# An issue list with 88 of 2459 operations in other places: an S4D convolution and a Hedgehog attention on one core

## The chip, the cores and the metric

The kernel runs on one core of a Trainium2 chip. The metric is the device time of one execution in microseconds (us). The core has five engines with an instruction queue each, and each takes its queue in order: PE (TensorE, matrix multiplication; the loading of its weights is shown apart as PEld), DVE (VectorE), ACT (ScalarE), POOL (GpSimd) and SP (SyncE, which here only issues DMA transfers). PE writes its results to PSUM, which has eight banks; DVE and ACT evict them from there.

## The reference, cut to what matters

Two heads work on inputs of their own and their outputs stand side by side, 2048 rows of 576 + 576 columns, in float32. Head A is a long convolution: a kernel K is summed out of 128 exponentials per channel, and FFTs of twice the length convolve it with u. Head B is linear attention with 32 heads of 18 columns.

```python
dt = jnp.exp(log_dt)                                        # A
A = -jnp.exp(log_A_real) + 1j * A_imag
C = (C_real + 1j * C_imag) * dt[:, None]
P = jnp.exp((A * dt[:, None])[:, :, None] * pos[None, None, :])
K = 2.0 * jnp.einsum("dn,dnl->dl", C, P).real
Kf = jnp.fft.rfft(K, L2)
Uf = jnp.fft.rfft(u_t, L2)
y = jnp.fft.irfft(Uf * Kf[None, :, :], L2)[:, :, :L]        # + u * D_skip
...
qkv = x @ wqkv                                              # B, split into q, k, v and heads
pq, pk = q @ w_phi, k @ w_phi
phi_q = concatenate([softmax(pq), softmax(-pq)])            # phi_k alike
kv, z = phi_k^T v, sum of phi_k
o = (phi_q kv) / (phi_q z + 1e-6)
out = concatenate([y, o @ wo])
```

## The kernel before, in words

The program first records 2459 operations in a plan (`Plan.op`), each with its engine (some with an alternate engine), the tiles that it reads and writes, and a number. An operation is one instruction, or one block of matmuls, or one transfer. `Plan.run` then walks through a long string, `ORDER`, and emits the operations in the order of its words; so the string sets what stands behind what in the queue of each engine. In a word the digits are the number of the operation; a trailing `x` takes the alternate engine; `@` and digits give the PSUM banks of the tiles that are made there; `:n` puts n matmuls on a tile of zeros in front of the operation (line 249, `self.zero.t` against 256 columns; they change no result). The semaphores follow from which tile an operation reads and writes.

What the operations are, in the order in which they mostly come:

- "fold" (lines 370 to 380): w_phi is multiplied into the weights. Four matmuls (line 375) and one more (line 376) for each of four stage tiles, named e, kvb, cs and e again, loaded from wkT; the other operand is fT. ACT copies the product as the high half (`wh`), DVE subtracts it to get the low half (`wl`) (lines 379 and 380). Operation 7 is the first block of four, operation 8 the one more of the same stage tile, operation 29 the next one more; 9 is the ACT copy of 7. 381 and 383 are such a block and its copy for the query weights.
- 16 "key" tiles of 128 rows: the projections (line 307, 14 matmuls of 288 columns for a half, weights `wh`/`wl` and, for v, `vh`/`vl`; operations 331, 198, 199, 158 and 159 are such halves), the two softmaxes on DVE, ACT and POOL (lines 446 to 470), and "k4", 64 small matmuls of e with v (line 508; operations 190, 229, 324, 150 and 170). The last product of the softmax is line 322, e<-e,small.
- 18 pairs of "group", which make K: "g0", six matmuls of 64 rows (line 811), "g1", range reduction and sines (lines 787 to 798), "g2", three exponentials of PSUM on ACT (line 824; 1511 and 1512 are two of them), "g3", four products on DVE (lines 828 to 833), and "g4", small matmuls (line 843; 1225, 1263 and 1517). Operation 1460 is a shift of a phase in g1, which either POOL (line 789) or ACT (line 787) can do.
- the transforms: "u" of the input, "kfirst" of K, 16 "product" steps that multiply the two (line 926 and elementwise steps; 2287 is the matmul block of product 13, 2339 an elementwise one of product 15), and 16 "last" steps (line 988), whose operand zi or cs is read back from DRAM by SP (line 979; 2445 for "last" 14, 2452 for 15) and whose result `ot` is stored (line 992).
- 16 "query" tiles: projection, softmax, transposes on PE (lines 562 and 590), the product with kv (line 578), division (line 326, o<-psum,small), and the output projection. 745 is a sum in the softmax of one of them (line 455), 752 and 754 evict the transposes of query 9.

The tile pools are small (three tiles for e, five for cs and ub, two for ff and zi), so a transfer or an eviction often waits for an earlier reader. On PE, the queue interleaves all these stages.

Of the kernel before, what the change touches and what calls it, by code (L numbers as in the profile page):

```python
# [1005 lines left out]
0 1 2 4 5 1104 1092 1105 6 1106 1107 1108 7@2:26 1109 1192 27 1110 8 34 9 1073 1095 1093 1111 20 51 13 1112 1113 1114 992 11 29@0 1115 1003 344 28  # L1006
36@6 35 21@4 12 30 37 52 1096 39 22 32 10 23 25 1094 44 15@2 1127 1116 1074 14 31 38 40 33 1004@06 1099 24 53 18 26 54 16 1154 19 1117 1137 287 1120
345 45 17 57@4 1075 1118 41 346x 1076 1077 56 46 1119 60 347 47 288 42 1078 289x 1005 349@2 1080 348 1121 290x 1122 61 1123 1124 1125 292@4 62 1161
291 1098 68 48 1126 1084 1128 268 43 1129 350@0 1396 1063 1138 1130 1006 1139 1131 1132 71 49 295 1133 1134 296 1400 1079 352 353 63 1135 58@6 1136 59
1081 55 3 64 354 1155 65 66 1082 351 1162 1156 69 67 72 355x 1085 1086 1140 73x 293@2 1157 50@4 1163 1193 361 1064@60 1007 269 1158 1194 356 1159 270x  # L1010
1083 70 297 271 74 1087 1097 294 298 1066 171 1088 304 1089 357 1164 299 300 77@0 358 301 272@2 1160 273 1165 303 1090 1399 276 1065 1091 1166 277 360
278 1401 1397 76 1199 111 1167 1200 80 302 1195 1147 1398 1168 1402 172 1141 274@2 359x 275 173x 305 1196 1142 81 1148 1197 362 174 1152@76 1201 82
279 1169 1170 1151@05 83x 285 1172 1067 1202 1171 1174 112 1203 113 79@2 1143 1175 1204 78 1180 75 1173 1068 280 1176 114 1177 1183 89 284 176@0
1153@23 1205 84 1198 1178@5 1149 85 325 1182 281 1181 1230 1207 86 175 1403 1038 177 1206 1231 1232 1179 282 1208 1233 115 283x 180 1234 117@6 1184
1185 116 286 1235 1186 1187@2 211 1048 181 120 179@0 1190@53 182 121 183 1237 326 1218 1150 87x 1238 1018 1221 1189@67 122 1188 178 327 1239 1209 1404
212 189 1211 328x 123x 88 118@2 330@0 119 213x 124 1210 1212 1213 1191@67 90 184 214 1214 129 1215 185 1220 188 1240 1144 1241 1216@5 1242 216@2 215
1145 1146 306 1269 91 1243 128 1236 1223 186 1268 187x 1224 1219 1222 92 1217 93 1405 1270 1271 331@6 219 220 94 332 1100 329 221 222 125 190 126 1419
1245 1406 333 1225@5 342x 1276 1275 1272 1277 1227@23 1244 1278 1246 1228@67 1247 334 127x 1249 1256 1226x 1248 191 335 223 218@0 1250 1252 1251 1253
217 1279 192 1280 193 130 1254@5 1273 307 228 1274 1259 336 194 1307 1049@20 1306 224 225 1051 1050x 341 1308 96@6 1282 1229@01 337 1281 1257 1258 97
1407 1262 338 197@2 339 100 101 196 1261 1260 199@6 308x 1052 1283 1284 198 226x 195 1412 227 1408 1409 1410 1411 1413 1255 200 1414 229 201 340x 1101  # L1020
# [5 lines left out]
318 254@0 1354 379x 133x 1333@62 1334 1335 1449 134 1439 151 1336 319 241 242 320 253 321x 1494 1495 246 1496 1497 257 258 256@6 1337@20 1338 259 1339  # L1026
324 1356@5 1499 1341@02 1343x 1453 1340 1489 260 243 244 152 153 154 1342 1490 1454 1455 255 266 261 1345@20 1344 1347 1346 136@6 1498 137 156@0 262
263 245 265 1348 140 141 1500 142 1019@26 1021x 424 157 1450 1020x 135 998 264x 267 160 1481@67 1501 1482@23 1503 1502 161 1504 143 1456 168 1457 162
144 248 1458 1459 163 1451 1461x 138@0 1507 164 1008 139 1506 1505 145 165 149 1357 1508@2 1452 363 999@60 380 1460x 1509 1510 1483@52:2 1000 382@6
1001x 381 383 146 1513 148 1511 1512 1002 1514 1515 166 158@0 401 147x 1516 385 159 384 169x 150 1517@5 167x 1518x 170 1034@20 1522 1523 1524 1525 386  # L1030
1526 366 1036x 1529 1443@54:2 1527 1530 1531 1532 1528 1533 1534 1462 1463 1022 1009@06:2 1011 1464 1035x 1444@23:4 403@6 1466 1467 402 1535 1445@54
1465 1472 1010 406 1468 404 394 1473 1043 1537 387 458 1469 1474 395@0 1536 1429 1470@2 396 408 1037 405 407 1471 1475 1476 389@6 388 1478 1477 1361
1362 397 392 365 390 409@2 399 410 1363 1364 1365 1366 411 1367 391 1479@5 1368 1369 1370 1371 1372 412 1480x 1430 1373 1374 413 400 414 367@4 393
371@5 368x 1013 994@62 398 995x 372x 1375x 1012 415 459@0 364 374x 996x 369x 460 373x 370x 461 462 463 375 1431 997 426@3 425 1538 1432 1376 416 417
1433 1044@16:2 1434 464 1435 1688 376 377 427 428 1377 1519@50:2 1539 1046 1045x 1520@41:2 155 1436 1541 429 526 492 418 465 1540 1542 1014@62:8 1545
1544 1521@54:4 1548 1437 430 1438 466 1543 431 432 1546@0 1653 1016 1550 1654 1549 1692 1551 1547 527@2 467 528 1655 1656 433 468 434 469 378 1015 419
435 436 439@1 1657 441@7 1554 437@0 470 1658 1552 1553 1358@56 440 1028 1555@4 1047 442 1659 1691 438 1378 1556 446@7 1379 1359@14 529 530 1667 531
1387 1381 1380 1382 447 448 1360@03 1661 1383 532 443@2 444 1660 1662 1384 1663 1388 1689 471@5 493@6 1664 533 445 1665 1690 1666 1668 534 1390 535
1385@2 472 1389 1386 473@5 449@14 475@2 420 474 1577 1391 450 536 1392 476 537 1393 421 538 494 495 451 496 480@5 1578 1017 1394@0 477@1 1395x 1579
# [68 lines left out]
```

## Time and profile before

| | us |
|---|---|
| median of 3 runs | 534.08 |
| lowest and highest | 532.86 and 534.81 |
| the profiled execution | 532.96 |
| span of its trace | 531.2 |
| PE busy / DVE busy | 516.0 / 450.5 |
| ACT busy / POOL busy | 381.2 / 344.3 |

The span is from the first instruction to the last; 1.8 us of the profiled execution lie around it. The mean granted clock of PE is 0.999 of full speed over the span. A row of the trace gives a start, a duration, engine, line and operation, and in brackets how long the engine was idle before it and what ended that. Matmuls overlap their neighbours, so the durations of single rows add up to more than the time between starts.

### The profile page before, as it was taken

How to read it: one execution, taken by the hardware profiler on the slowest of the kernel's cores; microseconds unless marked ns; L12 is line 12 of the kernel's file. 1: busy time of each engine (PE TensorE's matmuls, PEld its weight loads, DVE VectorE, ACT ScalarE, POOL GpSimd, SP SyncE). 2: the span in 40 equal slices, each digit the busy share in tenths (PEclk: the TensorE clock that was granted, in tenths of full speed). 3: DMA queues.
4: the chain of work that ended last, by engine and by line, in shares of the span. 5: the costliest groups of instructions: out<-in, count | busy, mean ns of one | idle time of the engine just before them, and what ended most of it. 6: DMA issues, size and time to landing. Idle time of an engine off the chain costs nothing.

```text
span 531.2 us, 19221 instructions
## 1 busy us (share of the span) xinstructions
PE 516.0 (97%) x8179; PEld 432.3 (81%) x8179; DVE 450.5 (85%) x705; ACT 381.2 (72%) x559; POOL 344.3 (65%) x483
## 2 busy tenths in 40 slices
PE   8999999999999899999999999999999999999997
PEld 7998999988988778988888666866788876776986
DVE  7999989797958798999999998999974899768641
ACT  6679979889568699899699978989733444354342
POOL 1167877957687957983659998896541526673233
PEclk9999999999999999999999999999999999999999
DMA  8836610425155666446762687765368699897884
GB/s 288 308 121 233 222 52 27 168 78 198 51 161 179 213 235 245 127 139 192 271 210 83 197 266 233 254 212 182 102 206 289 204 283 301 271 298 253 271 292 148
DMA packets 69900, 107.10 MB, mean 202 GB/s; under 512 B 5722, under 2 KB 49882, under 8 KB 69814
## 3 DMA queue, kind: packets, MB, share of 16 engines
q1 hardware_dynamic: 69174, 104.39, 60.3%
q0 software_dynamic: 640, 1.48, 0.9%
q8 instruction: 64, 1.05, 0.8%
q14 instruction: 22, 0.18, 0.1%
HBM read 61.30 MB, written 44.54 MB: 199 GB/s over the span
## 4 chain that ended last, share of the span: by engine, by line
PE 72%; DVE 14%; DMA 4%; issue 4%; ACT 4%; POOL 1%; SPq 0%; DVEq 0%; ACTq 0%; POOLq 0%
PE psum L307 67%; PE psum L562 3%; DMA ff<-in_ff_dram 2%; DVE cs L829 2%; DMA zi<-dram 1%; PE psum L590 1%; ACT psum L824 1%; DVE ac L326 1%; DVE small L447 1%; DVE small L455 1%; DVE cs L326 1%; DMA pa<-in_par_dram 1%; DVE e L326 1%; DVE cs L831 1%; DVE small L450 1%
## 5 line engine op out<-in xcount | busy, mean ns | idle before, releaser
L307 PE MATMUL psum<-vh,x 128*128 128x288 f32 x576 | 123.6, 301 | 0.2 <-DVE e L326 0.2
L307 PE MATMUL psum<-wh,x 128*128 128x288 f32 x576 | 123.6, 301 | 0.1
L770 POOL TENSOR_TENSOR cs<-cs,pi 128x32 int32<-128x32 int32 (+4 forms) x180 | 106.7, 598 | 7.6
L307 PEld LDWEIGHTS psum<-wh,x 128*128 128x128 f32 x576 | 94.3, 188 | 7.3 <-issue 3.7
L307 PEld LDWEIGHTS psum<-vh,x 128*128 128x128 f32 x576 | 94.0, 188 | 4.8 <-issue 3.2
L307 PE MATMUL psum<-wl,x 128*128 128x288 f32 x320 | 93.8, 296 | 0.0
L307 PE MATMUL psum<-vl,x 128*128 128x288 f32 x320 | 93.8, 295 | 0.0
L824 ACT ACTIVATE psum<-psum 128x512 f32<-128x512 f32 x108 | 59.0, 586 | 8.7 <-PE psum L307 8.1
L307 PEld LDWEIGHTS psum<-wl,x 128*128 128x128 f32 x320 | 60.2, 188 | 0.0
L307 PEld LDWEIGHTS psum<-vl,x 128*128 128x128 f32 x320 | 60.2, 188 | 0.0
L322 POOL TENSOR_TENSOR e<-e,small 128x1152 f32<-128x1152 f32 (+1 forms) x26 | 44.7, 1719 | 18.1 <-DVE small L326 12.9
L828 DVE TENSOR_TENSOR cs<-psum,cs 128x1024 f32<-128x1024 f32 x36 | 43.7, 1216 | 6.0 <-ACT psum L824 5.8
L322 POOL TENSOR_TENSOR x<-zo,x 64x128 fp32r<-64x128 f32 (+1 forms) x33 | 26.4, 804 | 32.2 <-ACT x L407 30.8
L322 POOL TENSOR_TENSOR e<-small,e 128x576 f32<-128x576 f32 x28 | 32.7, 1167 | 18.4 <-PE psum L307 7.8
L307 PEld LDWEIGHTS psum<-kvb,fT 126*128 126x128 f32 (+1 forms) x320 | 38.6, 188 | 7.2 <-issue 3.0
L829 DVE TENSOR_TENSOR cs<-psum,cs 128x1024 f32<-128x1024 f32 x36 | 43.6, 1215 | 0.9 <-ACT psum L824 0.8
L307 PE MATMUL psum<-kvb,fT 126*128 126x133 f32 (+1 forms) x320 | 42.0, 280 | 0.3 <-DVE ac L326 0.2
L307 PE MATMUL psum<-ub,ff 64*32 64x288 f32 x1024 | 40.4, 410 | 1.7 <-DMA ff<-in_ff_dram 0.6
L453 ACT ACTIVATE e<-e 128x1152 f32<-128x1152 f32 x32 | 37.4, 1168 | 6.4 <-POOL e L322 5.8
L307 PEld LDWEIGHTS psum<-cs 128*32 128x32 f32 x2304 | 34.0, 110 | 8.7 <-issue 2.2
L307 PE MATMUL psum<-cs 128*32 128x64 f32 x2304 | 39.7, 220 | 1.3 <-DVE cs L829 0.6
L312 ACT ACTIVATE zi<-psum 128x576 f32<-128x576 f32 x41 | 25.6, 649 | 20.4 <-PE psum L307 16.3
(157 smaller groups left out, 1134.2 us busy)
## 6 DMA issues: line engine op xcount, KB each, us to landing
dram<-zi SPq DMA_DIRECT2D x32, 576.0 KB
ub<-dram SPq DMA_DIRECT2D x64, 288.0 KB, 4.4
dram<-zo SPq DMA_DIRECT2D x32, 288.0 KB, 3.5
zo<-in_xT_dram SPq DMA_DIRECT2D x24, 320.0 KB, 4.0
zi<-dram SPq DMA_DIRECT2D x12, 576.0 KB, 6.9
ub<-in_u_dram SPq DMA_DIRECT2D x16, 288.0 KB, 4.9
xd<-x SPq DMA_DIRECT2D x8, 576.0 KB, 3.9
x<-xd SPq DMA_DIRECT2D x8, 576.0 KB, 5.9
```

The source lines that it names most:

```text
L307: pe.matmul(o, l, r, start=start, stop=stop, skip_group_check=skip)
L312: op(("act", "dve"), (c_act(n), c_dve(n)), lambda e: act.activation(dst(), src(), AF.Copy) if e == "act" else dve.tensor_copy(dst(), src() ...
L322: op(eng, [c_dve(n[0]) if e == "dve" else c_pool(n[1]) for e in eng], lambda e: (dve if e == "dve" else pool).tensor_tensor(dst(), a(), b( ...
L326: op(eng, c_dve(n) if eng == "dve" else c_pool(n), lambda: e.tensor_tensor(dst(), a(), b(), op=alu), r=r, w=w, with_=with_, lock=eng == "p ...
L447: op("dve", c_dve(D), lambda: dve.tensor_reduce(two(top.t), v(), axis=AX.X, op=ALU.max, negate=True), r=[p], w=[top])
L450: op("dve", c_dve(D), lambda: dve.tensor_reduce(rg.t, e.t[:, 0], axis=AX.X, op=ALU.min), r=[e], w=[rg])
L453: op("act", c_act(1152) + 40, lambda: act.activation(e.t, e.t, AF.Exp), r=[e], w=[e], table="exp")
L562: pe.transpose(tp.t[0:m, j - j0, :], e.t[:, sign, 7 * g:7 * g + GRP[g], :].rearrange("p h f -> p (h f)"), ident.t)
L770: op("pool", c_pool(2 * n * W), lambda n=n, j=j: pool.tensor_tensor(x()[:, :, :, n:2 * n], x()[:, :, :, 0:n], pi.t[:, j:j + 2, gs].bitcast ...
L824: op("act", c_act(512), lambda b=b: act.activation(b.t, b.t, AF.Exp), r=[b], w=[b], table="exp")
L828: op("dve", c_dve(64 * W), lambda: dve.tensor_tensor(F(), both(M.t), F(), op=ALU.mult), r=[M, cs], w=[cs])
L829: op("dve", c_dve(64 * W), lambda: dve.tensor_tensor(E.t[:, :, :, 32:64], both(up.t), cs.t[:, :, :, 0:32], op=ALU.mult), r=[up, cs], w=[E])
```

## The change: other places in the issue list

Only `ORDER` differs. 88 operations stand elsewhere, 4 of them transfers; 7 take another engine; the matmuls on zeros go from 105 to 117 (18 more in front of nine operations, 6 fewer in front of four others); some tiles take other PSUM banks. The engine changes are: 1460 (g1 of group 6) POOL to ACT, 1338 (an eviction of kfirst) ACT to DVE, 785 (a product of query 10) and 2339 (product 15) DVE to POOL, 2290 (an eviction of product 13), 752 and 754 DVE to ACT. The first lines of the string are:

```diff
-0 1 2 4 5 1104 1092 1105 6 1106 1107 1108 7@2:26 1109 1192 27 1110 8 34 9 1073 1095 1093 1111 20 51 13 1112 1113 1114 992 11 29@0 1115 1003 344 28
+0 2 1 4 5 1104 1092 1105 6 1106 1107 1108 1109 1192 27 1110 8@2 34 7:26 9 1073 1095 1093 1111 20 51 13 1112 1113 1114 992 11 29@0 1115 1003 344 28
```

On PE, the order changes in ten places. The first one is at the start of the program. PE's queue before ended its matmuls on zeros (26 pairs of a weight load and a matmul, from the first row on; the last two are shown) ahead of the fold:

```order
L249 LDWEIGHTS zero
L249 MATMUL psum<-ident,zero 128x256
L307 MATMUL psum<-fT,e 128x126 x10
L307 MATMUL psum<-fT,kvb 128x72 x5
L307 MATMUL psum<-fT,cs 128x126 x5
L307 MATMUL psum<-fT,e 128x126 x5
L307 MATMUL psum<-ub,w_161 128x288 x4
```

The first five rows of PE's queue now, up to the second of the 26 pairs:

```order
L1104 UNCONDITIONAL_BRANCH
L307 MATMUL psum<-fT,e 128x126
L249 LDWEIGHTS zero
L249 MATMUL psum<-ident,zero 128x256
L249 LDWEIGHTS zero
```

Operation 8, one matmul of the fold on the stage tile e, has moved from behind operation 7 to the head of the queue, and the 26 pairs stand behind it, still in front of operation 7.

Other places on PE: 331 has moved from between two other projection halves (`215 331 332 329 190 1225`) to between a k4 and a g4 (`215 332 329 190 331 1225`); likewise `196 199 198 229 1263` is now `196 229 198 199 1263`, `1337 324` is `324 1337`, and `158 159 150 1517` is `158 150 159 1517`.

On ACT, in the middle of the key tiles and groups 6 and 7, the queue before had one exponential, a copy of the query fold (wh, operation 383), and two exponentials (1511 and 1512):

```order
L824 ACTIVATE psum<-psum 128x512
L312 ACTIVATE zi<-psum 128x576
L379 ACTIVATE wh<-psum 128x4x126
L824 ACTIVATE psum<-psum 128x512 x2
L379 ACTIVATE wh<-psum 128x126
L794 ACT_TABLE_LOAD
L794 ACTIVATE cs<-cs 128x1040
```

The same place on ACT now:

```order
L824 ACTIVATE psum<-psum 128x512
L312 ACTIVATE zi<-psum 128x576
L824 ACTIVATE psum<-psum 128x512
L787 ACTIVATE cs<-cs 128x1040
L824 ACTIVATE psum<-psum 128x512
L379 ACTIVATE wh<-psum 128x4x126
L379 ACTIVATE wh<-psum 128x126
L794 ACT_TABLE_LOAD
L794 ACTIVATE cs<-cs 128x1040
```

1511 is no longer behind the fold's copy, and the shift 1460, which was on POOL, stands between 1511 and 1512.

On DVE, near product 13 and query 9, the queue before was (line 617 belongs to a query's output, line 322 is operation 2339, the first line 455 is operation 745, and line 579 starts a query's division):

```order
L326 TENSOR_TENSOR cs<-cs,psum 128x1152
L617 SCALAR_TENSOR_TENSOR zo<-zo,psum 128x576
L322 TENSOR_TENSOR cs<-cs 128x2x288
L455 TENSOR_REDUCE small<-o 128x2x32
L579 RECIPROCAL small<-psum 128x11
L579 RECIPROCAL small<-psum 128x21
L326 TENSOR_TENSOR o<-psum,small 128x198
L326 TENSOR_TENSOR o<-psum,small 128x378
L467 RECIPROCAL small<-small 128x32
L312 COPY cs<-psum 128x2x288
```

The same place on DVE now:

```order
L326 TENSOR_TENSOR cs<-cs,psum 128x1152
L617 SCALAR_TENSOR_TENSOR zo<-zo,psum 128x576
L579 RECIPROCAL small<-psum 128x11
L579 RECIPROCAL small<-psum 128x21
L326 TENSOR_TENSOR o<-psum,small 128x198
L326 TENSOR_TENSOR o<-psum,small 128x378
L455 TENSOR_REDUCE small<-o 128x2x32
L467 RECIPROCAL small<-small 128x32
```

2339 has gone to POOL, 745 stands behind the division, and the copy to cs (2290) has gone to ACT.

On SP, the load 2445 of zi for "last" 14 now stands ahead of the load 2452 of cs for "last" 15, and three stores stand elsewhere.

## Rows read from the trace of the kernel before

**Rows 1.** The page: busy time by engine, and the chain that ended last, by engine.
```profile
PE 516.0 (97%) x8179; PEld 432.3 (81%) x8179; DVE 450.5 (85%) x705; ACT 381.2 (72%) x559; POOL 344.3 (65%) x483
...
PE 72%; DVE 14%; DMA 4%; issue 4%; ACT 4%; POOL 1%; SPq 0%; DVEq 0%; ACTq 0%; POOLq 0%
```

**Rows 2.** Busy time by stretch: sum, PE, PEld, DVE, ACT, POOL; granted clock, DMA share.
```profile
13.00:52.00 39.00, 38.59 (x461) 36.57 (x459) 38.44 (x62) 30.13 (x39) 20.82 (x40) 1.00 0.64 227
52.00:165.00 113.00, 112.98 (x1978) 102.22 (x1979) 96.26 (x131) 93.65 (x122) 86.52 (x129) 1.00 0.39 128
...
215.00:296.00 81.00, 80.78 (x1227) 67.72 (x1229) 78.15 (x139) 72.05 (x109) 58.50 (x91) 1.00 0.51 160
```

**Rows 3.** Line 249 alone in two stretches: PE busy and count, PEld, clock.
```profile
1.47:4.60 3.13, 3.13 (x15) 2.25 (x16) 1.00 0.82 245
4.90:6.10 1.20, 1.20 (x11) 0.84 (x9) 1.00 0.90 299
```

**Rows 4.** The timeline, 0 to 12 us: PE's first work.
```profile
1.47 4.64 PE L249 MATMUL psum<-ident,zero 128*128 128x256 bf16 x26 [1.47 <-DVE zero L345]
...
6.09 2.42 PEld L307 LDWEIGHTS psum<-fT,e 126*128 126x128 f32 x20 [0.26 <-DVE pa L326]
6.12 2.58 PE L307 MATMUL psum<-fT,e 126*128 126x126 f32 x20
```

**Rows 5.** The timeline of PE, 82 to 93 us, around operation 331.
```profile
84.72 0.30 PE L307 MATMUL psum<-vh,x 128*128 128x288 f32 x1
...
86.58 0.29 PE L307 MATMUL psum<-wh,x 128*128 128x288 f32 x1
...
88.54 0.72 PE L307 MATMUL psum<-e,v 128*19 128x36 f32 x62
```

**Rows 6.** The timeline, 172 to 185 us, around operations 1511, 1460 and 170.
```profile
174.29 1.92 POOL L789 TENSOR_TENSOR cs<-cs,quarter 128x1040 int32<-128x1040 int32 x1
...
175.14 0.59 ACT L379 ACTIVATE wh<-psum 128x504 fp32r<-128x504 f32 x1 [1.47 <-PE psum L307]
...
175.63 1.08 ACT L824 ACTIVATE psum<-psum 128x512 f32<-128x512 f32 x2
...
176.26 1.23 DVE L829 TENSOR_TENSOR cs<-psum,cs 128x1024 f32<-128x1024 f32 x1 [0.84 <-ACT psum L824]
...
178.21 1.07 ACT L794 ACTIVATE cs<-cs 128x1040 f32<-128x1040 int32 x1
...
178.68 2.19 POOL L322 TENSOR_TENSOR e<-e,small 128x1152 f32<-128x1152 f32 x1 [0.26 <-DVE small L463]
...
180.93 0.39 PE L307 MATMUL psum<-e,v 128*19 128x36 f32 x23 [0.53 <-POOL e L322]
...
182.17 0.55 PE L307 MATMUL psum<-e,v 128*19 128x36 f32 x41 [0.85 <-issue]
```

**Rows 7.** The timeline, 444 to 454 us, around operations 2339 and 2287.
```profile
446.41 2.38 DVE L322 TENSOR_TENSOR cs<-cs 128x576 f32<-128x576 f32 x1
...
446.72 1.44 POOL L322 TENSOR_TENSOR zo<-zo 128x576 f32<-128x576 f32 x1
...
449.65 0.79 DVE L326 TENSOR_TENSOR o<-psum,small 128x198 f32<-128x198 f32 x2
...
450.04 1.17 PE L307 MATMUL psum<-ub,ff 64*32 64x288 f32 x16 [0.54 <-DVE o L326]
...
450.84 1.42 POOL L322 TENSOR_TENSOR cs<-cs 128x576 f32<-128x576 f32 x1
```

**Rows 8.** The timeline, 495 to 505 us: SP's loads for "last" 14 and 15, and PE.
```profile
496.00 0.43 SPq L979 DMA_DIRECT2D cs<-dram  x1
496.53 1.58 SPq L979 DMA_DIRECT2D zi<-dram  x2
...
503.61 0.72 PE L307 MATMUL psum<-zi,w 64*32 64x288 f32 x16 [0.51 <-DMA zi<-dram]
```

**Rows 9.** PE's waits, in groups: us in total, times, longest.
```profile
PE psum L249 <- DVE ac L326: 1.0, 1, 1.0
```

More of the change, by code (lines that the diff above doesn't have):

```diff
@@ L1040 @@
+1385@0 472 1389 1386 473@5 449@14 475@0 420 474 1577 1391 450 536 1392 476 537 1393 421 538 494 495 451 496 480@5 1578 1017 1394@0 477@1 1395x 1579
 1669 1580 1585 1584 1581 481 1557 452 1582 1558@26 482 1560 1586 543@0 478 1694 479 483@51 1559x 1561 1053 1587 1588 1589 544 1590 497 1441 453
@@ new lines @@
+2162@6 1741 1723 1724 1725 1726 1751 2048 491 2157 567 1742 2160@4 517@01 557 2161 2163 568 518 1612@45 519 1743 558 606 1633 520 630@6 1632 569 1753
+1613@02 521 1614@31 1641 1635 570 1634 629 1636 1744 1752x 1638 1637 2047 1643 522@4 1642 2164 2165 2046 1732 2054 2131 1754 1639@0 1783 1784 1785
+1786 631 523 1644 1727 632 2051@6 607@2 1646 571 1787 1728 1788 1789 1640x 1647 1645 1735@03 1648@1 1777 1776 1755 2052x 524x 1778 1756 2166@64 608
+1649 1779 1791x 2167 1736@12:2 1758 1759 2168 1757 1764 611@0:2 1780 1781 609@3 1761 1734 1782 1760 2049@4:2 610 612 2053 1737@36 1790x 2050 2110
@@ new lines @@
+2004 1817x 585@01 586 587 2000@6 2001 1844 1733 2123 1837 1810 588 589 2124@24 2125 2126 1845x 2002@6 2006@0 2008@4 1945 1846x 2003 2007 2009 2012
+2010 2011 1818 624@6 2014x 625 2127 1947 626x 1803@20 2130 1805x 1811@46 1847 1812x 1804 1813 2013 2015@20 636 2132 1826@6 2129 2138 2128 637 2137
+2016 1827 1948 1949 2135@4 2133@6 2090 1950 1952 1953 2017 1954 2018x 2136 2141@4 2022x 1955 2134 2020x 2142 2019 1956 2139@6 2021 525 1828@23 590@0
+1848 2089 2140 1829@46 1849 2095 1851 1852 1830@57 1850 1853 1957 1958 1951 591 663@2 2023 1959 1854 1857 1860 2144 1960x 638 2143 1855@4 592x 1858
@@ new lines @@
+664 1859 1915 639 1862 1961 2088 1914 1916 1863 1917 1861 665 666 667 2093@0 2091@6 2092 1856 1864@5 1814 2094 2096 2097@6 1918 640 1919 2024 696 1920
+2099@2 697 1865x 627 2145@04 2098 1907 668 1942@67:1 1962 2100 2075 1943@32:3 1908 2146 2069 1963 643@4 669 698 1909 1964 1965 641@5 642 645@6 699
+2147 700@0 644 1944@54 1966 1971 1967 1968 1974 1910 1973 2102 2101 1969@7 646 701 1806 1911 1972 1922 1970 670 1912 671 2033 1913 1976 1921 2067 2148
+2149 2068 1977 672 1975 2074 593 2150 673 674 2103@62 2104 702 1877 1978@4 703 1876 2070@2 1870 1869 2025 2072@0 647@5 2026 1878 2027 1979x 2071x
@@ new lines @@
+744 2258 2285 832@2 2393x 890 829@3 2338 2286 803@4 2259 2284 833 2392 830 834 2383@6 891 831 2384 2289@0 2287@2 2260 2291 745 2339 835@67 746 2290
+836 837 747 2288 804 838 2292 2261 839 892 893 894 2395 2340 2341@02 805 2293@6 748 2262 2342 2295@4 2361 2380 895 751@3 753@2 2313 2343 2306 754 752
+841@0 749@3 2296 2294 2305 2310@4:1 2308@6 750 2311 2309 2312 2316@2 758@5 2344 2314@6 2317 2297 2345 755@4 2265 2315 2298 2346 759 756 760 2299@26
+757 806 896 918 919 920x 761@45 762 840 2270 2379x 763 2300 2388 2264 2381x 2348@6 764 2319 921 899@4 2301 2318 842 2378 2263 765 2266@2 900x 2267
@@ L1089 @@
+2413 2428 953 954 2427 987 2404@4 2405x 2408x 2409x 2407 2406 988@6 989 990 991
 """
```

118 lines of the change are left out of this document (50 added, 68 removed).

## The prediction, as it was put on record

> **What bounds the kernel now.** I read the page first: PE is busy for 516.0 of 531.2 us, and the chain that ended last runs on PE for 72% of the span [rows 1]. So PE's queue is the bound, and a change of order counts where it makes PE idle, makes it idle less, or makes it work longer. The next view was the busy time in stretches. From 13 to 52 us PE is idle for 39.00 − 38.59 = 0.41 us, from 52 to 165 us for 0.02 us, from 215 to 296 us for 0.22 us [rows 2]. In these stretches nothing that another engine gains can show, and what is added to PE is paid. Over the whole span PE's idle time is 531.2 − 516.0 = 15.2 us, of which 1.47 us lie ahead of its first instruction [rows 4]; the rest, some 13 us, lies almost wholly behind 165 us. There the timeline and the list of PE's waits show short stalls of 0.2 to 1.0 us, each with another releaser. The edits behind 165 us are to be held against these stalls one by one.
>
> **The start.** Before, PE runs its 26 matmuls on zeros from 1.47 us for 4.64 us, and the fold's matmuls follow at 6.12 us; its weight load had waited 0.26 us [rows 4]. The zeros therefore cost nothing: they lie in the wait for the first stage tile e, which has landed by 6.09 us. Their pace is worth a look. The first 15 take 3.13 us, 0.209 us each, the last 11 take 1.20 us, 0.109 us each [rows 3]. A matmul of 256 columns in 0.109 us is PE at the upper of its two levels, 2.4 GHz; 0.209 us is the lower one, 1.2 GHz. The profile gives a granted clock of 1.00 for both stretches, so I go by the pace.
>
> After, operation 8 stands first. It reads the same tile e, so it can't start before about 6.1 us, and all 26 zeros are behind it in an in-order queue, ahead of operation 7. What was filler in a wait is now work in the way of the fold. PE has then done nothing for 6.1 us, as it had done nothing before 1.47 us, so I take the same course for the block: 4.64 us. Operation 8 itself has only moved. So operation 7 and all behind it on PE come 4.6 us later. The bounds: 26 × 0.109 = 2.8 us if the upper level holds from the first, 26 × 0.209 = 5.4 us if it never comes within the block.
>
> The Trainium skill ("TensorE: Matmul & The Clock Gate", the section "Part 1: The HAM clock gate") says that the throttled level is the default, that activity releases it, and that the point of release moves from run to run. By that rule the new order is the worse one, as by the rows; that the point moves is shown by no run here. With it the block could cost anything between the two bounds above.
>
> How much of this is swallowed? From 6.12 us to 165 us PE has 0.41 + 0.02 us of idle time to give [rows 2]. A stall can shrink only if what it waits for doesn't come later too. The softmax steps that end these small stalls hang on projections made on PE, so they come later too, but not all their work does; I let the whole 0.4 us go. **Start: 4.6 − 0.4 = +4.2 us** (2.4 to 5.4).
>
> **The moved projection halves and small matmuls, 80 to 180 us.** Two projection halves behind one another start 86.58 − 84.72 = 1.86 us apart; from such a half to a k4 behind it there are 88.54 − 86.58 = 1.96 us [rows 5]. A change of shape costs about 0.10 us. Operation 331 is now alone between k4 and g4, the pair 198 and 199 too; each gives two more such changes, and the g4 behind comes after a large block where it came after a k4. With operation 324, where only the neighbours change, I count six changes: **+0.6 us** (0.2 to 0.8), paid in full because PE has no idle time there [rows 2]. Operation 150 lies beside a stall of PE and costs nothing while that stall stands.
>
> **The zeros elsewhere.** 12 more, at 0.109 us each, are at most +1.3 us [rows 3]. Most of the new ones lie where PE is full, between 215 us and shortly behind 296 us [rows 2], and one where zeros wait 1.0 us already [rows 9]; the last costs nothing, since it lies in the wait. A zero in a short stall is free, in a full stretch it is paid unless a stall behind it shrinks. I take a third: **+0.4 us** (0 to 1.3).
>
> **Around 180 us.** DVE's product of line 829 waits 0.84 us for an exponential on ACT, since that stood behind the fold's copy, for which ACT waited 1.47 us on PE [rows 6]. With 1511 ahead of the copy, DVE's wait goes. The shift 1460, 1.92 us on POOL, goes to ACT, where an operation on 128x1040 takes 1.07 us [rows 6]; it fits in the 1.47 us that ACT waited. POOL's last softmax product, 2.19 us from 178.68 us, for which PE waits 0.53 us and behind which comes an issue gap of 0.85 us [rows 6], can start when POOL and the reciprocal on DVE let it, both some 0.8 us or more earlier. The lower bound is 0.4 us (the wait alone, most of it), the upper 0.53 + 0.85 = 1.4 us. I take **−0.9 us**, between the two, since the gap at issue may stay: no row says what it hangs on. What is late next is the eviction behind operation 159, which now comes after k4.
>
> **Around 449 us.** PE waits 0.54 us for the division on DVE, and the block then takes 1.17 us [rows 7]. DVE is late because 2339 took 2.38 us there, while POOL ran an operation of the same size from 446.72 us; the like on POOL took 1.42 us [rows 7]. With 2339 on POOL and 745 behind the division, DVE reaches the division 2.4 us and the time of 745 earlier, so the wait goes whole; the block itself, stretched by its late operands, may lose as much again. Bounds 0.5 and 1.1 us; **−0.9 us**. POOL must now do 2339 ahead of a query's sum; the cover is POOL's own idle time there. If that fails, the query's softmax is 1.4 us late, and PE would wait some of it at the next transposes.
>
> **Around 503 us.** PE waits 0.51 us for zi, issued at 496.53 us behind the load of cs at 496.00 us [rows 8]. Issued first, it starts 0.5 us earlier; **−0.4 us** (0 to 0.5), because both loads then share the transfer engines still.
>
> **The rest.** 785 to POOL, 752 and 754 to ACT, 1338 to DVE, bank numbers and three stores: the waits near them end on PE or on loads, so I take zero, with 0.5 us either way. The cover of 752 and 754 is ACT's idle time late in the program; without it each is an eviction of some 0.4 us more on the path.
>
> **Sum.** 4.2 + 0.6 + 0.4 − 0.9 − 0.9 − 0.4 + 0 = **+3.0 us**. The profiled execution takes 532.96 us, so 536.0 us by that; it lies 1.1 us under the median of 534.08 us. Against the median the forecast is **537.1 us**, 0.56% more. A difference of 0.5% (2.67 us, so 531.4 to 536.75 us) is about what can be told from no change here.
>
> **Rivals.**
>
> *The upper level comes at once.* Operation 8 and the loads of weights ahead count as activity, or the state is another after 6 us. The start is then 2.8 − 0.4 = 2.4 us and the sum +1.2 us: 535.3 us, no change. For it: the clock column says 1.00 throughout [rows 3]. Against: the pace of the first 15. The same would follow if half of the zeros' time were swallowed somewhere.
>
> *The shift is swallowed late.* PE idles for some 13 us behind 165 us. If half of these stalls end on something that doesn't hang on the early PE work (loads, POOL's and DVE's own chains), 2 to 4 us of the 4.2 go there: 533 to 535 us. Against: the longer stalls end on softmax products and evictions of PSUM, which PE's own work feeds.
>
> *Faster: the stretches behind 165 us are paced by DVE and POOL, not by PE.* Then the start doesn't reach the end at all, and what counts is what DVE and POOL are relieved of on their chains: 1.92 us on POOL near 174 us, 2.38 us on DVE near 446 us, 0.5 us for zi; with +0.6 and +0.4 on PE the sum is −3.8 us: 530.3 us. It decides if POOL's softmax product in front of operation 170 ends by about 179 us although PE began 4.6 us later. For it: DVE is busy for 78.15 of 81.00 us from 215 to 296 us [rows 2]. Against: PE is full there too, with 0.22 us idle.
>
> *Slower still: everything on PE is paid.* The block at 5.4 us with nothing swallowed, 0.8 us for the shapes, all 1.3 us of zeros, and only the lower bounds of the gains (0.4 + 0.5 + 0): +6.6 us, 540.7 us; halfway to it 539 us.
>
> **How the numbers follow.** The forecast has a chance of 0.40, with 535.8 to 538.6 us as its own range, of which 0.05 lies under 536.75 us; the clock rival 0.21, the swallowed shift 0.15, the faster one 0.11, the slower one 0.13. Slower by over 0.5%: 0.35 + 0.13 = 0.48. Within: 0.05 + 0.21 + 0.15 = 0.41. Faster: 0.11. For the range I leave out the faster rival and half of the slowest, 0.17 together: 532.4 to 539.6 us.
>
> **What would show it.** In the changed kernel's timeline, PE's first instruction should be one matmul of the fold at about 6.1 us, then 26 zeros of some 4.6 us in all, and the rest of the fold at about 10.9 us. Operation 170, which began at 180.93 us [rows 6], should begin at about 184 us: 4.2 and 0.6 us later, less its wait and the gains in front of it. If it begins near 182.5 us, the clock rival holds; if the start is late but operation 170 isn't, the faster one. Operation 170's wait of 0.53 us, the 0.54 us ahead of operation 2287 and the 0.51 us ahead of "last" 14 should be gone or below 0.2 us. The forecast is wrong if the first stage tile lands later than the zeros would end anyway, or if new stalls behind 180 us, where ACT has more to do, take the place of those removed.

## The result, and the profile after

The changed kernel took 540.49 us (median of 4 runs, 539.88 to 540.95), the kernel before 534.44 us beside it: ratio 1.0122, 95% interval [1.0096, 1.0149], so 6.5 us slower, with an interval from 5.1 to 8.0 us (the two medians alone lie 6.05 us apart). The forecast was 537.1 us, range to 539.6. The direction was right, the size about half. The profiled execution took 540.61 us, its span 538.8 us, 7.6 us more than before.

The page of the changed kernel, busy time by engine:

```profile
PE 517.1 (96%) x8191; PEld 434.5 (81%) x8191; DVE 447.2 (83%) x701; ACT 383.0 (71%) x562; POOL 347.2 (64%) x484
```

Against [rows 1], PE works 1.1 us more; the other 6.5 us are idle time. PE's waits in the changed kernel (total, times, longest) say where:

```profile
PE psum L307 <- DVE pa L326: 6.0, 1, 6.0
PE psum L307 <- DVE x L322: 3.3, 1, 3.3
```

The first is the start, foreseen. The second is new and was in no part of the prediction. The start, in the timeline of PE:

```profile
5.99 0.76 PE L307 MATMUL psum<-fT,e 126*128 126x126 f32 x2 [5.99 <-DVE pa L326]
6.54 4.77 PE L249 MATMUL psum<-ident,zero 128*128 128x256 bf16 x26
11.15 2.17 PE L307 MATMUL psum<-fT,e 126*128 126x126 f32 x18
```

Operation 8 begins when the zeros of [rows 4] had ended, the block takes 4.77 us, and the fold goes on at 11.15 us: 5.0 us later than in [rows 4]. Then the stall, in the same view some 30 us on:

```profile
42.50 0.29 PE L307 MATMUL psum<-wh,x 128*128 128x288 f32 x1
42.63 0.30 PE L307 MATMUL psum<-wl,x 128*128 128x288 f32 x1
46.22 0.53 PE L307 MATMUL psum<-wh,x 128*128 128x288 f32 x2 [3.29 <-DVE x L322]
...
48.06 0.45 PE L307 MATMUL psum<-wh,x 128*128 128x288 f32 x1
48.30 0.45 PE L307 MATMUL psum<-wl,x 128*128 128x288 f32 x1
```

Operation 77, the projection of key tile 1, waits for its operand x, the last part of which DVE makes (operation 73). Behind the stall the pace changes: two starts are 0.13 us apart at 42.5 us and 0.24 us at 48.06 us. The stretches of the changed kernel behind it (sum, then busy time of PE, PEld, DVE, ACT and POOL; granted clock):

```profile
46.10:49.40 3.30, 3.18 (x18) 3.18 (x19) 3.30 (x5) 3.30 (x7) 1.57 (x3) 0.74 0.39 151
49.40:52.00 2.60, 2.60 (x16) 2.60 (x15) 0.89 (x3) 2.58 (x4) 2.04 (x1) 0.67 0.63 196
```

After 3.3 us without work PE went on, and from about 47.8 us it ran for part of the time at the lower level, 1.2 GHz: the granted clock is 0.74 and 0.67 in the two stretches behind the stall. The next projection half needs 51.29 − 48.06 = 3.2 us where it took 1.86 us [rows 5], 1.4 us more.

Why is operation 73 late? DVE's timeline in the kernel before, in which the two rows x<-zo,x are 73 and then 270, the row L663 is operation 1083, and the reduction in the last row is 297:

```profile
34.48 1.07 DVE L326 TENSOR_TENSOR cs<-ac,cs 128x640 fp32r<-128x640 f32 x1
35.48 0.81 DVE L326 TENSOR_TENSOR pi<-pi,ot 128x384 f32<-128x384 f32 x1
36.22 1.28 DVE L322 TENSOR_TENSOR x<-zo,x 128x512 fp32r<-128x512 f32 x2
37.42 0.81 DVE L663 SCALAR_TENSOR_TENSOR ac<-ac,ldc 128x640 f32<-128x640 f32 x1
38.15 0.74 DVE L450 TENSOR_REDUCE small<-e 128x32 f32<-128x576 f32 x1
```

and in the changed kernel, where 297 has gone ahead of operation 67 (a move on DVE that the section on the change does not list, nor that of 73), and the two rows x<-zo,x are 270 and then 73:

```profile
36.79 0.70 DVE L450 TENSOR_REDUCE small<-e 128x32 f32<-128x576 f32 x1
...
40.76 1.79 DVE L326 TENSOR_TENSOR cs<-ac,cs 128x640 fp32r<-128x640 f32 x1
42.47 0.96 DVE L322 TENSOR_TENSOR x<-zo,x 128x512 fp32r<-128x512 f32 x1
43.35 1.72 DVE L663 SCALAR_TENSOR_TENSOR ac<-ac,ldc 128x640 f32<-128x640 f32 x1
45.00 1.17 DVE L322 TENSOR_TENSOR x<-zo,x 128x512 fp32r<-128x512 f32 x1
```

Two things differ. 73 stands behind 270 and 1083. And the same four instructions (operation 1085, 270, 1083, 73) take 1.79 + 0.96 + 1.72 + 1.17 = 5.6 us instead of 1.07 + 1.28 + 0.81 = 3.2 us. POOL in the kernel before:

```profile
38.98 1.17 POOL L322 TENSOR_TENSOR e<-small,e 128x576 f32<-128x576 f32 x1 [2.94 <-DVE small L450]
```

POOL in the changed kernel:

```profile
40.66 1.21 POOL L322 TENSOR_TENSOR e<-small,e 128x576 f32<-128x576 f32 x1
...
41.89 3.73 POOL L770 TENSOR_TENSOR cs<-cs,pi 128x128 int32<-128x128 int32 x3
```

Before, POOL waited 2.94 us for 297, and DVE had these microseconds to itself. With 297 early, POOL's softmax product (operation 298) and its phase steps run beside them.

The three gains that were forecast came, as the rows of PE's timeline in the changed kernel show. Around 180 us operation 170 begins at 190.08 us, 9.15 us later than in [rows 6], while the block ahead of the moved ones began 9.4 us later; its wait on POOL is gone, the gap at issue is still 0.71 us. Around 449 us the block of product 13 takes 1.2 us for its two halves, with no wait in it, where [rows 7] have 1.17 us for one half behind a wait of 0.54 us. Near the end zi is there in time, and PE waits for it no more:

```profile
190.08 0.38 PE L307 MATMUL psum<-e,v 128*19 128x36 f32 x21
191.17 0.57 PE L307 MATMUL psum<-e,v 128*19 128x36 f32 x43 [0.71 <-issue]
...
458.14 1.18 PE L307 MATMUL psum<-ub,ff 64*32 64x288 f32 x32
...
511.22 0.71 PE L307 MATMUL psum<-zi,w 64*32 64x288 f32 x16
```

### The profile page after: what moved, and what is told of

Same layout as the page of the kernel before. It is cut to its first block, busy times and chain, and to the rows that moved or that the text cites. A ratio compares the mean times of both kernels' runs of the same rounds, so it can differ in the third digit from the quotient of the medians.

```text
span 538.8 us, 19244 instructions
## 1 busy us (share of the span) xinstructions
PE 517.1 (96%) x8191; PEld 434.5 (81%) x8191; DVE 447.2 (83%) x701; ACT 383.0 (71%) x562; POOL 347.2 (64%) x484
## 3 DMA queue, kind: packets, MB, share of 16 engines
q8 instruction: 64, 1.05, 0.8%
## 4 chain that ended last, share of the span: by engine, by line
PE 79%; DVE 11%; ACT 5%; issue 2%; DMA 2%; POOL 1%; SPq 0%; DVEq 0%; ACTq 0%
PE psum L307 72%; PE psum L562 3%; PE psum L249 2%; PE psum L590 1%; DVE cs L829 1%; DVE ac L326 1%; DVE cs L326 1%; ACT psum L824 1%; DMA pa<-in_par_dram 1%; DMA ff<-in_ff_dram 1%; ACT wh L379 1%; DVE x L322 1%; DVE small L447 1%; DVE vl L396 1%; ACT L824 1%
## 5 line engine op out<-in xcount | busy, mean ns | idle before, releaser
L307 PE MATMUL psum<-wh,x 128*128 128x288 f32 x576 | 125.2, 303 | 3.5 <-DVE x L322 3.3
L770 POOL TENSOR_TENSOR cs<-cs,pi 128x32 int32<-128x32 int32 (+4 forms) x180 | 108.4, 608 | 7.6
L322 POOL TENSOR_TENSOR e<-e,small 128x576 f32<-128x576 f32 (+1 forms) x27 | 45.9, 1698 | 20.5 <-DVE small L326 13.9
```

What stands on the lines that cost most here:

```text
L307: pe.matmul(o, l, r, start=start, stop=stop, skip_group_check=skip)
L322: op(eng, [c_dve(n[0]) if e == "dve" else c_pool(n[1]) for e in eng], lambda e: (dve if e == "dve" else pool).tensor_tensor(dst(), a(), b( ...
L770: op("pool", c_pool(2 * n * W), lambda n=n, j=j: pool.tensor_tensor(x()[:, :, :, n:2 * n], x()[:, :, :, 0:n], pi.t[:, j:j + 2, gs].bitcast ...
```

## The experiments

Each run is compared with runs of the kernel before on the same chip (medians 533.1 to 533.9 us); ratios with their 95% intervals. In the diffs, the words of the issue list stand as they do in the string, with "..." for what is not touched. Single runs of one kernel lie up to 7 us apart, and the intervals are 0.9 to 1.6 us wide to either side, so a difference of about 1 us is not told from none.

**The start undone in the changed kernel.**

```diff
-8@2 34 7:26 9
+7@2:26 8 34 9
```

> The changed kernel with only the start put back: the 26 matmuls on zeros ahead of operations 7 and 8. My theory: the loss is two costs that add up, the block of zeros in the way of the fold (4.7 us) and operation 73 behind 1083 on DVE (a stall of PE of 3.3 us and some 1.3 us at the lower level behind it). So this gives 540.5 - 4.7 = 535.8 us, and the stall ahead of operation 77 stays at about 3.3 us. Rival, one cause: the late start piles up DVE's work and makes the stall; then the stall goes with the start and this gives about 531.5 us.

537.62 us (534.69 to 541.9), ratio 1.0066 [1.0036, 1.0097]: 1.8 us over the expectation, with runs 7 us apart. Its timeline of PE has the stall unchanged but for the 4 us by which it is earlier:

```profile
41.95 0.69 PE L307 MATMUL psum<-wh,x 128*128 128x288 f32 x2 [3.06 <-DVE x L322]
```

So the start did not make the stall; the rival with one cause falls.

**Operation 73 put back in the changed kernel.**

```diff
-355x 1086 1140 293@2 ... 70 271 73x 74
+355x 1086 1140 73x 293@2 ... 70 271 74
```

> The changed kernel with only operation 73 (DVE's part of loading key tile 1) put back to its place behind 1140, ahead of 1085, 270 and 1083. My theory: the stall ahead of operation 77 goes (3.3 us) and with it the pace at the lower level behind it (1.3 us), less 0.4 us of small stalls that come back: 540.5 - 4.2 = 536.3 us. Rival, one cause (the start): DVE is late anyway, the stall moves to operation 272 or stays, and the time stays over 539.5 us.

540.37 us (540.29 to 540.73), ratio 1.0126 [1.0099, 1.0153]: nothing gained. My theory was wrong here. 73 is early now, but in PE's timeline the stall stands one place further on, ahead of operation 272:

```profile
47.83 0.40 PE L307 MATMUL psum<-wh,x 128*128 128x288 f32 x1 [3.07 <-ACT v L312]
```

Operation 272 waits for a PSUM bank that ACT frees with operation 304 (v, line 312). In ACT's in-order queue 304 is behind 1088, which reads what DVE's 1083 writes (ac); in the changed kernel 1083 is done at 43.35 + 1.72 = 45.07 us. ACT's timeline in the changed kernel (1088, then 304):

```profile
45.16 0.74 ACT L315 ACTIVATE cs<-ac 128x640 fp32r<-128x640 f32 x1 [3.32 <-issue]
45.80 0.63 ACT L312 ACTIVATE v<-psum 128x576 f32<-128x576 f32 x1
```

The view names no releaser for 1088; that it is 1083 follows from the tile and from the start 0.09 us behind its end (0.08 us in the kernel before).

In the kernel before these two rows begin at 38.31 and 38.96 us, and 304 ends at 39.60 us; PE began operation 272 at 39.65 us. The list of waits shows nothing there, but there was no slack either: in the runs with a visible wait for 304 PE also begins 0.05 to 0.06 us behind its end.

**Start and operation 73 both put back.** The diff is that of the two runs above together.

> The changed kernel with the start and operation 73 both put back. My theory, two costs that add: 540.5 - 4.7 - 4.2 = 531.6 us, under the kernel before (534.4), since the rest of the change then gains some 2.8 us. Rival, that the rest of the change gains nothing by itself and what looks like its gain is a stall that shrinks because PE comes later: 534 us.

536.1 us (533.38 to 539.42), ratio 1.0052 [1.0029, 1.0076], 4.5 us over the expectation: the stall of 3.0 us ahead of 272 is here too. The start is worth 540.37 − 536.1 = 4.3 us by this pair, and 540.49 − 537.62 = 2.9 us by the changed kernel and the first run.

**Zeros in the stall.**

```diff
-50@4 1163 1085 361 1064@60
+50@4 1163 1085 361 1064@60:24
```

> The changed kernel with 24 more matmuls on zeros (2.6 us) in front of operation 1064, some 4 us ahead of the stall of 3.3 us in front of operation 77. My theory: the stall ends when DVE ends operation 73, so the zeros only take its place (0.7 us of it stays), and PE doesn't fall to the lower level: 540.5 - 1.3 = 539.2 us, with halves behind the stall 1.86 us apart instead of 3.2. If the slow pace behind the stall is not from PE's idleness, 540.5 us. If the stall isn't set by DVE, 543 us.

540.34 us (539.63 to 543.13), ratio 1.0131 [1.0104, 1.0157]: nothing gained, although the stall is gone, the pace behind it is full and PE begins operation 1266's block at 120.3 us, 2.5 us earlier. What became of the 2.5 us is followed below.

**Operation 297 put back in the changed kernel.**

```diff
-65 66 297 1082 ... 1083 70 271 73x 74
+65 66 1082 ... 1083 70 271 73x 297 74
```

> The changed kernel with only operation 297 put back behind the loads: DVE does it behind 1085, 270, 1083 and 73 again, 73 stays where the change put it. Theory A (POOL's overlap): 297, moved ahead, lets POOL start 298 and the phase steps behind it while DVE does 1085, 270, 1083 and 73, and the two engines stretch one another (0.7 to 0.8 us each became 1.0 to 1.8); 1083 is late, so ACT's 1088 and 304, and PE's bank. With 297 back POOL idles beside them, they take 0.7 to 0.8 us again, the stall of 3.3 us and the slow pace behind it go: 540.5 - 4.2 = 536.3 us. Theory B (DVE's order alone): 73 behind 270 and 1083 is what is late; the stall stays over 2 us and the time over 539 us.

536.53 us (535.63 to 541.63), ratio 1.0058 [1.0033, 1.0082], as theory A had it, with 73 still behind 1083. DVE's timeline (operations 1085, 270, 1083, 73):

```profile
40.23 1.08 DVE L326 TENSOR_TENSOR cs<-ac,cs 128x640 fp32r<-128x640 f32 x1
41.24 0.68 DVE L322 TENSOR_TENSOR x<-zo,x 128x512 fp32r<-128x512 f32 x1
41.84 0.81 DVE L663 SCALAR_TENSOR_TENSOR ac<-ac,ldc 128x640 f32<-128x640 f32 x1
42.58 0.68 DVE L322 TENSOR_TENSOR x<-zo,x 128x512 fp32r<-128x512 f32 x1
```

All four have their old durations, 3.2 us together, and PE's wait ahead of 77 is 0.38 us.

**POOL early, in the kernel before.**

```diff
-298 1066 ... 357 1164 299 ... 1160 273 1165
+1164 1160 1165 298 1066 ... 357 299 ... 273
```

> The kernel before, with three of POOL's phase steps (1164, 1160, 1165) ahead of 298 instead of behind it, so that POOL works while DVE does 73, 270 and 1083; DVE's order is that of before. Theory A: these three stretch from 0.7 or 0.8 us to over 1.0 us each, 1083 ends 1 to 2 us later, 304 on ACT too, and PE waits about as long ahead of operation 272: 534.2 + 1.2 = 535.4 us, a stall of 1 to 2 us where there was 0.1. Theory B: DVE's order is as before, so no stall and 534 us.

DVE's order is that of before, only POOL's differs. In its timeline the two x<-zo,x (73 and 270) take 2.38 us instead of 1.28, 1083 takes 1.09 instead of 0.81, and PE waits 1.3 us ahead of 272, as theory A had it:

```profile
36.48 2.38 DVE L322 TENSOR_TENSOR x<-zo,x 128x512 fp32r<-128x512 f32 x2
38.78 1.09 DVE L663 SCALAR_TENSOR_TENSOR ac<-ac,ldc 128x640 f32<-128x640 f32 x1
```

The time does not show it: 534.27 us, ratio 0.9999 [0.9981, 1.0018]. A stall of 1.3 us, of which two small stalls behind it give back 0.2 to 0.4, lies at the edge of that interval; so this run shows that the overlap makes the stall, not what it costs (534 us was theory B's time).

**The start alone, in the kernel before.** On PE the edit is the first one's reverse.

> The kernel before with only the start of the change: operation 8 at the head of PE's queue, the 26 matmuls on zeros between it and operation 7. As predicted: 4.6 us on PE less 0.4 swallowed, 534.2 + 4.2 = 538.4 us, and no stall near 40 us. Rival, that the shift is swallowed behind 165 us: under 536.5 us.

539.02 us (537.27 to 541.26), ratio 1.0092 [1.0065, 1.0119], 4.9 us. The block of zeros takes 5.04 us in its profile. No stall near 40 us. The two small stalls at 50.6 and 56.4 us are there as before (0.19 and 0.23 us): nothing of the shift was swallowed.

**The rest alone:** the changed kernel with start, 73 and 297 put back.

> The changed kernel with the start, operation 73 and operation 297 put back: the rest of the change alone. By the terms as predicted (+0.6 shapes, +0.4 zeros, -0.9, -0.9, -0.4): 534.2 - 1.2 = 533.0 us, no stall near 40 us. If other moves near the start cost something too, 535 us or more.

531.6 us (530.75 to 533.91), ratio 0.9966 [0.9948, 0.9985], 1.8 us less than before and faster than both kernels, and 1.4 us better than expected. No stall near 40 us.

**The rest without its costs:** as the last, and 18 zeros fewer and the four blocks of PE back.

```diff
-332@6 ... 190 331 ... 196 1261 1260 ... 229 198@6 199 201 ... 324 1337@20 ... 138@0:2
+331@6 219 ... 332 ... 190 ... 196 1261 1260 199@6 ... 198 ... 229 201 ... 1337@20 324 ... 138@0
```

> The rest alone (as in the run before, 531.6 us), and in it the 18 added matmuls on zeros left out and operations 331, 198, 199 and 324 back at their old places on PE: what is left are the moves around 180, 449 and 503 us and the bank numbers. As predicted, the shapes cost 0.6 us and the zeros 0.4 us: 530.6 us. If these two terms are nothing, 531.6 us; if the zeros do something useful in a stall, over 532 us.

530.97 us (530.19 to 533.12), ratio 0.9956 [0.9936, 0.9975]: the lowest of all. It lies 0.1 points, 0.5 us, under the run before; that is inside both intervals, so the two terms of 1.0 us together are neither shown nor refuted by the times. The profile of the run before also has a stall at issue of 0.60 us, at 306 us, that this one has not.

**Operation 297 ahead, alone, in the kernel before.**

```diff
-66 1082 ... 1083 70 297 271
+66 297 1082 ... 1083 70 271
```

> The kernel before with one operation moved: 297 on DVE, from behind 1083 to ahead of 67, as in the change. Theory A (POOL's overlap): 1085, 73, 270 and 1083 take 1.0 us or more each where they took 0.7 to 1.1, ACT's 304 is some 2.5 us late, PE waits 2.5 us ahead of operation 272 and goes on at the lower level: 533.9 + 3.5 = 537.4 us. Theory B (the place of 73): no stall over 1 us, 534.5 us at most.

534.78 us (533.1 to 539.87), ratio 1.0036 [1.0011, 1.0061]: 1.9 us, half of the expectation, and a stall of 1.7 us where 2.5 were expected, with no fall of the pace behind it in the profiled run, which is the fastest of the twelve. Theory B had no stall over 1 us. DVE's timeline of this kernel, operations 73, 270 and 1083:

```profile
36.05 1.65 DVE L322 TENSOR_TENSOR x<-zo,x 128x512 fp32r<-128x512 f32 x1
...
37.63 0.84 DVE L322 TENSOR_TENSOR x<-zo,x 128x512 fp32r<-128x512 f32 x1
38.40 1.74 DVE L663 SCALAR_TENSOR_TENSOR ac<-ac,ldc 128x640 f32<-128x640 f32 x1
```

and POOL's timeline beside it:

```profile
35.95 1.21 POOL L322 TENSOR_TENSOR e<-small,e 128x576 f32<-128x576 f32 x1
37.12 0.81 POOL L770 TENSOR_TENSOR cs<-cs,pi 128x64 int32<-128x64 int32 x1
...
37.89 1.57 POOL L770 TENSOR_TENSOR cs<-cs,pi 128x512 int32<-128x512 int32 x1
```

POOL's three end at 37.16, 37.93 and 39.46 us; DVE's three end at 37.70, 38.47 and 40.14 us, which is 0.54, 0.54 and 0.68 us later, a little less than each of them takes alone (0.68, 0.68, 0.81). The rows read as if DVE does not slow down but stands still until POOL's instruction is done and then takes its normal time. That 297 itself takes DVE's time ahead of the loads is not the reason: 73 begins at 36.05 us here and at 36.22 us in the kernel before.

**Operation 73 behind, alone, in the kernel before.**

```diff
-1140 73x 293@2 ... 297 271 74
+1140 293@2 ... 297 271 73x 74
```

> The kernel before with one operation moved: 73 on DVE, behind 270, 1083 and 297 as in the change. Theory A: POOL idles beside them as before, 73 ends some 2 us later than it did, PE waits 1.2 us ahead of operation 77, less what the small stalls behind it give back: 533.9 + 0.8 = 534.7 us. Theory B: a stall of 3 us and 537 us.

533.24 us, ratio 1.0000 [0.9984, 1.0016], with a wait of 0.4 us ahead of 77 where theory A had 1.2. No cost of 73's place by itself is seen; theory B's stall of 3 us isn't there.

**Zeros again**, 20 instead of 24; 20 in the kernel with start and 73 put back; and 16 in the kernel before with 297 ahead.

```diff
-1064@60
+1064@60:20
```

> The changed kernel with 20 matmuls on zeros in front of operation 1064 instead of the 24 of the earlier run, which shifts the program behind them. If the clock's share of the stall (PE 2.5 us earlier at 120 us with 24 zeros) was given back by stalls at issue that depend on where the instructions happen to lie, this comes out near 538.5 us. If PE's early work is swallowed whatever the layout, 540.3 us again.

> The changed kernel with the start and operation 73 put back (297 still ahead; 536.1 us), and 20 matmuls on zeros in front of operation 1064, which fill 2.1 us of the stall of 3.0 us ahead of operation 272. If the lower level behind the stall costs 1.4 us of the end time: 534.7 us, with halves 1.87 us apart behind a stall of some 0.9 us. If PE's time there is swallowed or given back later, as in the two runs with zeros before: 536 us or more.

> The kernel before with operation 297 ahead (534.8 us, a stall of 1.7 us and no fall of the level) and 16 matmuls on zeros in front of operation 1064, 1.7 us, which fill that stall. The zeros only take its place: 534.8 us. If matmuls on zeros do harm by themselves further on (their place in the program, not their time), 536 us or more.

542.26 us, ratio 1.0159 [1.0133, 1.0185]; 537.59 us, 1.0070 [1.0044, 1.0096]; and 535.48 us, 1.0029 [1.0011, 1.0047]. None can be told to be faster than the same kernel without zeros (1.0122, 1.0052, 1.0036), and the first is slower than either of its two expectations. In the profile of the first, PE is 2.5 us ahead of the changed kernel at 120 us, 0.95 us ahead at 381 us, and 1.75 us behind at 389 us. The last step is a fall of the clock; the busy times of that stretch (columns as above):

```profile
382.00:390.00 8.00, 7.50 (x104) 5.05 (x89) 6.28 (x8) 4.63 (x10) 4.25 (x4) 0.60 0.48 150
```

It does not explain the time of this kernel: the profiled run, with a mean granted clock of 0.992, took 542.1 us, and the five others, with 0.999 to 1.000, took 540.99 to 542.92 us.

In PE's timeline of the second, a stall at issue of 1.0 us stands at 336 us, at operation 2139:

```profile
336.61 0.67 PE L307 MATMUL psum<-ub,ff 64*32 64x288 f32 x3 [1.00 <-issue]
```

The three kernels that have 20 or 24 zeros there and the rest of the change all have a stall at issue at this operation (0.38, 0.54 and 1.0 us) and one of 0.2 to 0.3 us at operation 235; the changed kernel and the ones with no zeros there have none at either, though some of them have one of 0.6 to 0.8 us elsewhere, at 306 to 312 us. The time lost at such a place is more than its wait. This is operation 2139 in the changed kernel, and then with 24 zeros:

```profile
339.01 1.27 PE L307 MATMUL psum<-ub,ff 64*32 64x288 f32 x32 [0.28 <-ACT ac L312]
```

```profile
337.29 1.24 PE L307 MATMUL psum<-ub,ff 64*32 64x288 f32 x25 [0.28 <-ACT ac L312]
338.91 0.69 PE L307 MATMUL psum<-ub,ff 64*32 64x288 f32 x7 [0.38 <-issue]
```

It begins 1.72 us earlier than in the changed kernel and ends 0.68 us earlier, so 1.0 us of the lead is gone. Between the same matmuls of the two traces the lead with 24 zeros is 2.5 us up to 139 us, 1.9 us at 146 us, 1.7 us from 195 to 337 us, 0.7 us at 345 us and 0.15 us at 408 us. So the two operations with the new stalls at issue take 1.6 us of the 2.5, and 0.6 us go behind 403 us.

What a stall at issue hangs on can be counted in the traces. The 16 of them have 34 such stalls of 0.2 us or more on PE, the one near 180 us in every kernel among them. Each of the 34 stands behind the same number of PE's instructions, 193, beyond a multiple of 256 (weight loads, matmuls and the few others of its queue). And each ends 1.2 to 1.6 us behind the landing of a transfer on the queue that the page of the changed kernel lists with 64 transfers and 1.05 MB, one for every 256 of PE's 16,382 weight loads and matmuls:

```profile
q8 instruction: 64, 1.05, 0.8%
```

So PE waits there for its next block of instructions. Zeros added ahead move the place: with 24 of them the stall stands before the last 7 matmuls of operation 2139, with 20 before the last 3. Most of the 64 places show no stall; no run here tests what makes the difference.

## Why the prediction was wrong

**The step that failed is "The rest"**, the zero in the sum for all edits without a term of their own, "with 0.5 us either way", and before it the reading of the full stretches: "In these stretches nothing that another engine gains can show, and what is added to PE is paid." That sentence speaks of gains, and I took it to mean that DVE's and POOL's order ahead of 165 us doesn't matter. A loss elsewhere does show: PE is full there, but its operands and banks come with little slack. In the kernel before, operation 73 ended 0.8 us ahead of its use, and the bank of operation 272 was freed with no slack at all. The move of 297 had no term and stands nowhere in the prediction. It makes POOL run beside DVE, which then waits for POOL instruction by instruction, and the lateness goes by way of DVE's 1083, ACT's 1088 and 304, and a PSUM bank to PE; where 73 stands behind 1083, PE stalls one place earlier, ahead of 77. That the overlap makes the stall is shown from both sides: with 297 back the durations return and the stall goes, with POOL early and DVE's order untouched the durations stretch and PE waits 1.3 us.

The sign of it stood in rows that the prediction used. In [rows 7] DVE's 2339, 2.38 us from 446.41 us, ends at 448.79 us, 0.63 us behind the end of POOL's row (446.72 + 1.44 = 448.16 us). I read the 2.38 us as its own length; four operations of its size on DVE take 734 ns in the mean:

```profile
L322 DVE TENSOR_TENSOR ac<-ac 128x576 f32<-128x576 f32 x4 | 2.9, 734 | 0.0
```

What 297's place costs is shown by three pairs that differ in 297 (some in 73 too, which alone cost nothing that can be seen): in the kernel before 0.36 points of ratio, 1.9 us; with the rest of the change 1.0052 − 0.9966 = 0.86 points, 4.6 us; with rest and start 1.0122 − 1.0058 = 0.64 points, 3.4 us. The smallest price goes with a stall of 1.7 us, the larger ones with stalls of 3.0 to 3.3 us and a fall of the level behind them. Each ratio is known to 0.2 or 0.3 points, so the three prices are not told apart, and the part of the lower level in them is not shown.

**The start** was right in its mechanism and a little small. Forecast +4.2; measured 4.9 us alone in the kernel before (interval 3.5 to 6.4), 2.9 and 4.3 us in the two pairs of the changed one. The block took 4.77 us in the changed kernel and 5.04 us in the run of the start alone (forecast 4.64, bounds 2.8 and 5.4). The part that failed is "I let the whole 0.4 us go": in the run of the start alone the small stalls at 45 and 51 us moved along, by some 5 us each. The clock rival (2.8 us for the block) and the swallowed shift fall with the run of the start alone.

**The rest without 297 and 73**: forecast 0.6 + 0.4 − 0.9 − 0.9 − 0.4 = −1.2 us, measured −1.8 us with an interval from −2.8 to −0.8. The three stalls that the gains were to remove went, as the rows in the section on the result show. The gain around 180 us was under its term, about the wait of 0.4 us, because the gap at issue stayed; "no row says what it hangs on", the prediction said, and the count above says that it is one of the places where PE waits for instructions. Shapes and zeros, 1.0 us together, are of the size of what the times can tell; the run without them is 0.5 us lower, inside the interval.

**The sum.** Start 0.92, 297 0.64 and rest −0.34 points make 1.22 points, the ratio measured. That they fit to the last digit is luck: other pairs of these runs give 0.56 to 0.92 points for the start and 0.36 to 0.86 for 297. The forecast had 4.2 − 1.2; what was missing is 297 (3.4 us) and 0.7 us at the start, and the rest was better by 0.6 us.

**The slower rival** ("everything on PE is paid", 540.7 us) has the right time for the wrong reason: the block did not take 5.4 us, and the gains were not at their lower bounds. **The faster rival** asked whether operation 170 keeps its time though PE began late; it came 9.15 us later, so that rival falls, and the run of the start alone keeps its shift (5.1 us at its two small stalls, 4.9 us at the end). But the runs with zeros show that a lead of PE is not passed on in the same way.

What stays open: whether the 1.4 us that the lower level takes behind the stall go on to the end. The three runs that filled the stall with zeros gained nothing by the end. The runs of the changed kernel itself say no more than that: one of the four has a mean granted clock of 1.000 and took 540.37 us, the three others, with 0.996 and 0.997, took 539.88 to 540.95 us.

## What to carry to other kernels

A stretch in which PE shows no wait says nothing on how near the next wait is: for each move on another engine, take the end of what it delays and the start of who uses it, and write the slack down; here it was nothing and 0.8 us. An instruction moved ahead on one engine also releases its consumer on the next, and the question is what that consumer will then run beside. Filler work is free only on the side of the wait on which PE would be idle; moved to the other side of the operation that waits, all of it is paid. And whatever adds or takes PE instructions moves the places where PE waits for its next block of them, which at one operation here was worth 1.0 us; a difference of that size need not come from what was changed.

## What the runs showed of the hardware

DVE's elementwise operations on two tiles in SBUF wait for a POOL operation in full: beside one they ended 0.54 to 0.68 us behind its end, whatever the duration that shows in their row (0.84 to 1.74 us). The Trainium skill ("SBUF — State Buffer", section "SBUF: two separate sides") says so: DVE and GpSimd share a pair of ports, taken for a whole instruction by the one that comes first. The trace agrees for a DVE operation behind one of POOL. DVE's reductions, which read one tile, kept their time: in the changed kernel one takes 1.34 us from 46.09 us, with POOL busy from 45.69 us for 1.45 us, as long as the one at 34.94 us.

PE went on at full pace after the stall of 1.7 us in the profile with 297 ahead. Behind the stalls of 3.0 to 3.3 us it ran at the lower level: from the first matmuls on in the two profiles with the start put back, and from 1.6 us into the work in the changed kernel, where one run of four shows a granted clock of 1.000 and so no such fall. In one run the clock fell near 382 us (granted clock 0.60 from 382 to 390 us), behind four waits of 0.2 to 0.5 us between 376 and 381 us; the changed kernel has the same four waits, and a granted clock of 1.00 there. At the start of the kernel before the column of the granted clock says 1.00 while the pace is half [rows 3], so the pace of equal matmuls is the surer reading there.

A stall of PE at issue stood in all 34 cases at a fixed count of PE's instructions, one place in every 256, and ended 1.2 to 1.6 us behind the landing of a transfer of instructions.

The 26 matmuls on zeros at the start take between 4.55 and 5.70 us in the profiles of these kernels, whether they stand first or behind operation 8, so the point at which their pace changes moves.
